# Packed attention and an expert layer on one core: weight staging in shared places, loads five pieces ahead, and PSUM pairs shared by h, W' and attention

## The chip, the core and the metric

The kernel runs on one core of one Trainium2 chip. The core has a matrix engine (TensorE, PE in the profile, with its weight loads as PEld), VectorE (DVE), ScalarE (ACT), GpSimd (POOL) and SyncE (SP), which here only issues DMA transfers. PE writes into PSUM, which has eight banks of 512 float32 values in each of 128 partitions; ACT and DVE read it from there. Every engine works through its own queue in order and waits on semaphores for the others. The metric is the device time of one execution in microseconds (us), and the number compared is the median of the runs.

## The reference

Batch 8, 8 heads, 576 tokens, head size 64, 32 packed queries a head. All inputs are float32 except the two weights, which reach the kernel as float64 (512 x 2048 and 2048 x 512).

```python
def sm_attn(qq, kk, vv):
    s = scale * np.matmul(qq, kk.transpose(0, 1, 3, 2))
    s = s - np.max(s, axis=-1, keepdims=True)
    a = np.exp(s)
    a = a / (np.sum(a, axis=-1, keepdims=True) + 1e-09)
    return np.matmul(a, vv)
p_packed = sm_attn(p, k, v)
out = sm_attn(q, p_packed, p_packed)
...
h = x @ w_in
sp = np.maximum(h, 0.0) + np.log1p(np.exp(-np.abs(h)))
g = h * erf(sp)
return (g @ w_out).astype(np.float32)
```

x is the attention's output with its heads side by side: 4608 tokens of 512 values.

## The kernel before

**Algebra.** The second attention of a batch has only 32 keys a head, so its output is never formed. `w_prime(b, j)` multiplies the packed values of batch b with 512 columns of w_in and gives W'; an h block then multiplies W' with the attention weights a2 of the batch. Float32 precision comes from splitting each factor into a high and a low float32r part and adding three products (`wph` x `a2h`, `wph` x `a2l`, `wpl` x `a2h`); the same holds for g x w_out (`woh`, `wol`, `gh`, `gl`).

**Units.** The work is cut into 128 units (b, c, i): batch b, half c of its tokens (288), and 256 of the 2048 hidden values (i of 8). `h_block` (lines 399 to 439) makes h of a unit: two halves k, each six matmuls into one PSUM bank, evicted by ACT. `o_block` (445 to 472) multiplies g by w_out and accumulates in four banks (`ps_o`) over the i of a segment; then ACT copies them out (L466) and a DMA writes them. For the first 32 units (batches 0 and 1, grouped) the gate is softplus and erf, each behind a table load, taken for two or three units at a time (lists `ENDS`, functions `begin_gates` and `end_gates`); h is copied at L417, and o runs five units behind h. For the other 96 the gate is a chain of tanh and square (L429 to L438), h is evicted at L419, and o runs three units behind. The first eight units use w_out whole, unsplit (`whole`).

**Weights.** A float64 piece of 128 x 512 comes by DMA into a staging tile of 4 KB a partition (L87). `begin` scales its upper words on ACT (L93), `end` repairs the bits with three DVE passes (L96 to L98). There are 16 pieces of w_in, `("wi", j, c)`, and 16 of w_out, `("wo", f)`; `split_w_out` (`"sp"`) later makes `woh` on ACT (L114) and `wol` on DVE (L115). Staging has two places (pool `stage`); the third to eighth load borrow places of the W' pool (`EARLY`), two more borrow places of a2. All loads, k, v, q and most output stores go through SP's queue.

**Order.** The opening is written out by hand (lines 582 to 655): attention of batch 0 (`first`, in the output banks) and of batch 1 (`second`) are generators that are stepped between weight conversions, filler matmuls (`keep_busy`) and the first four h blocks, and `keep_order` fixes that order on PE, DVE, ACT and SP. After it, `plan` says which conversions, attention steps, W' and splits are traced after which h block: `("wo", 4)` to `("wo", 7)` after h 4 and h 5, the others spread over h 7 to 16. From there the framework's scheduler orders each queue. In `do`, an item `"wi"` or `"wo"` issues its transfer and then at once traces its conversion.

**PSUM.** Eight banks: four in `ps_o`, two single ones in `ps_h` (one half of h each), and one pair in `ps_m`, used in turn by W' and by the attention's scores, transposes and packed output. The tile names in the profile are h, wp, s, t, p and o; `wos` and `wi` are staging tiles, `wo` and `w_in_sb` the float32 weights.

Of the kernel before, what the change touches and what calls it, by code (L numbers as in the profile page):

```python
# [28 lines left out]
def tile_pack_attention_moe(ctx: ExitStack, tc: tile.TileContext, qT, kT, v, pT, w_in, w_out, outT):  # L29
    nc = tc.nc  # L30
    P = 128
    B, _, NC, S = qT.shape
    DFF = w_in.shape[1]
    DM = w_out.shape[1]
    HT = S // 2
    NDM = DM // P
    FB = 512
# [16 lines left out]

    FIRST = {4: [("wo", 4), ("wo", 5)], 5: [("wo", 6), ("wo", 7)]}
    LATER = (7, 17)
    ENDS = (1, 3, 5, 7, 9, 12, 15, 18, 21, 24, 27, 29, 31)

    EARLY = ("wpl", "wpl", "wph", "wph", "wpl", "wpl")

    cpool = ctx.enter_context(tc.tile_pool(name="const", bufs=1))
    apool = ctx.enter_context(tc.tile_pool(name="attn", bufs=2))
    opool = ctx.enter_context(tc.tile_pool(name="wo", bufs=2 * (DFF // P) + 1))
    spool = ctx.enter_context(tc.tile_pool(name="stage", bufs=2))
    wpool = ctx.enter_context(tc.tile_pool(name="wp", bufs=NFB))
    tpool = ctx.enter_context(tc.tile_pool(name="tmp", bufs=3))
    ps_o = ctx.enter_context(tc.tile_pool(name="ps_o", bufs=1, space=bass.MemoryType.PSUM))
    ps_h = ctx.enter_context(tc.tile_pool(name="ps_h", bufs=2, space=bass.MemoryType.PSUM))
    ps_m = ctx.enter_context(tc.tile_pool(name="ps_m", bufs=1, space=bass.MemoryType.PSUM))

    ident = cpool.tile([P, P], F32, name="ident")
    bias = cpool.tile([P, 4], F32, name="bias")
    w_in_sb = cpool.tile([P, 4, DFF], F32, name="w_in_sb")
    wo, wo_hi, wo_lo = {}, {}, {}
# [2 lines left out]
    for i, c in enumerate((T_BIAS, Q_BIAS, U_BIAS, A_BIAS)):  # L77
        nc.vector.memset(bias[:, i:i + 1], c)

    def load_f32(dst, src, name, pool=None, tag="wst"):  # L80

        if src.dtype == F32:
            nc.sync.dma_start(dst, src)
            return (lambda: None,) * 2
        n = src.shape[1]
        st = (pool or spool).tile([P, n], I64, name=name, tag=tag)
        nc.sync.dma_start(st[:], src)  # L87
        words = st[:].bitcast(U32).rearrange("p (n two) -> p n two", two=2)
        low, high = words[:, :, 0], words[:, :, 1]
        bits = dst.bitcast(U32)  # L90

        def begin():
            nc.scalar.mul(dst, high.bitcast(F32), F64_SCALE)  # L93

        def end():
            nc.vector.tensor_scalar(bits, bits, 3, None, op0=ALU.logical_shift_left)  # L96
            nc.vector.scalar_tensor_tensor(bits, high, 0x80000000, bits, op0=ALU.bitwise_and, op1=ALU.bitwise_or)  # L97
            nc.vector.scalar_tensor_tensor(bits, low, 29, bits, op0=ALU.logical_shift_right, op1=ALU.bitwise_or)  # L98

        return begin, end  # L100

    def load_w_in(j, c, **slot):
        return load_f32(w_in_sb[:, c, j * FB:(j + 1) * FB], w_in[c * P:(c + 1) * P, j * FB:(j + 1) * FB],
                        f"wi{j}_{c}", **slot)

    def load_w_out(f, **slot):
        made = opool.tile([P, DM], F32, name=f"wo{f}", tag="wo")
        wo[f] = made
        return load_f32(made[:], w_out[f * P:(f + 1) * P, :], f"wos{f}", **slot)

    def split_w_out(f):
        hi = opool.tile([P, DM], F32R, name=f"woh{f}", tag="wo")
        lo = opool.tile([P, DM], F32R, name=f"wol{f}", tag="wo")
        nc.scalar.copy(hi[:], wo[f][:])  # L114
        nc.vector.tensor_tensor(lo[:], wo[f][:], hi[:], op=ALU.subtract)  # L115
        wo_hi[f], wo_lo[f] = hi, lo

    functions = []
# [11 lines left out]
    wp = {}  # L130
# [4 lines left out]
    def attention(b, roomy=False):  # L135
# [5 lines left out]
        def chunk(name, tag="kvq"):  # L141
            if tag == "kvq":
                return apool.tile([P, S], F32, name=f"{name}_{b}", tag="kvq", bufs=6)[:]
            return tpool.tile([P, S], F32, name=f"{name}_{b}", tag=tag)[:]

        def bank(name):

            if name in at_o:
                d = at_o[name]
                return [ps_o.tile([P, 512], F32, name=f"{name}_{b}_{x}", tag=f"ps_o{d + x}")[:] for x in range(2)], None  # L150
            ps = ps_m.tile([P, 2, 512], F32, name=f"{name}_{b}", tag="ps_m")
            return [ps[:, 0, :], ps[:, 1, :]], ps

        def copy_out(dst, banks, n):
# [10 lines left out]
        k = [chunk(f"k{c}") for c in range(NC)]  # L165
# [5 lines left out]
        for j in range(NCH):  # L171
            n = min(P, S - j * P)
            nc.sync.dma_start(values[j][0:n, 0:2 * NC * 64], v[b, j * P:j * P + n, :])
        yield
        q_at = ("t0", "t0", "t0", "t1") if roomy else ("kvq",) * NC
        q = []

        def load_q():
            q.extend(chunk(f"q{c}", q_at[c]) for c in range(NC))
            for c in range(NC):  # L180
                nc.sync.dma_start(q[c], qT[b, :, c, :])

        if b != 1:
            load_q()
            yield
        a1 = apool.tile([P, 2, S], F32, name=f"a1_{b}", tag="big", bufs=3)
        scores = []
        for c2 in range(2):
# [54 lines left out]
        for j in range(NCH):  # L243
            n = min(P, S - j * P)
# [7 lines left out]
        (nc.scalar.copy if roomy else nc.vector.tensor_copy)(ptt[:], po[:, 0:P])  # L252
        pt[b] = ptt
        yield
        if b == 1:
            load_q()
            yield
# [91 lines left out]
    def w_prime(b, j):  # L349

        hi = wpool.tile([P, 2, FB], F32R, name=f"wph{b}_{j}", tag="wph")
        lo = wpool.tile([P, 2, FB], F32R, name=f"wpl{b}_{j}", tag="wpl")
        ps = ps_m.tile([P, 2, 512], F32, name=f"wp{b}_{j}", tag="ps_m")
        for c in range(NC):
            for r in range(2):
                nc.tensor.matmul(ps[NK * c:NK * c + NK, r, :], pt[b][64 * r:64 * r + 64, NK * c:NK * c + NK],  # L356
                                 w_in_sb[64 * r:64 * r + 64, c, j * FB:(j + 1) * FB], start=True, stop=True)
        nc.scalar.copy(hi[:], ps[:])
        wp[b, j] = (hi, lo)
        return lambda: nc.vector.tensor_tensor(lo[:], ps[:], hi[:], op=ALU.subtract)  # L360
# [38 lines left out]
    def h_block(b, c, i, whole, n):  # L399


        grouped = n < GROUPED
        hs = tpool.tile([P, 2, HT], F32, name=f"hs{b}_{c}_{i}", tag="t1" if grouped and sum(n > e for e in ENDS) % 2 else "hs")
        for k in range(2):
            f = (2 * i + k) * P
            j, fo = f // FB, f % FB
            whi, wlo = wp[b, j]
            ps = ps_h.tile([P, 512], F32, name=f"h{b}_{c}_{i}_{k}", tag="ps_h")
            m = 0
            ahi, alo = a2[b]  # L410
            for r in range(2):
                for w, a in ((whi, ahi), (whi, alo), (wlo, ahi)):
                    nc.tensor.matmul(ps[:, 0:HT], w[:, r, fo:fo + P], a[:, r, c * HT:(c + 1) * HT],  # L413
                                     start=(m == 0), stop=(m == 5))
                    m += 1
            if grouped:
                nc.scalar.copy(hs[:, k, :], ps[:, 0:HT])  # L417
            else:
                nc.scalar.mul(hs[:, k, :], ps[:, 0:HT], 0.5)  # L419
        if grouped:  # L420
            group.append((hs, b, c, i, whole))
            if n in ENDS:
# [95 lines left out]
    for k, (b, j) in enumerate(uses):  # L518
# [5 lines left out]
        n = ready[b]  # L524
# [10 lines left out]
    conversions = [0]  # L535

    def fetch(what, *which, **slot):
        if not slot:
            conversions[0] += 1
        if not slot and 2 < conversions[0] <= 2 + len(EARLY):  # L540
            slot = dict(pool=wpool, tag=EARLY[conversions[0] - 3])
        return (load_w_in if what == "wi" else load_w_out)(*which, **slot)

    def do(items):
        for it in items:
            if it[0] == "att":
                b = it[1]
                if b not in gens:
                    gens[b] = attention(b)
                next(gens[b])  # L550
            elif it[0] == "sp":
                split_w_out(it[1])
            elif it[0] in ("wi", "wo"):
                for step in fetch(*it):
                    step()
            else:
                w_prime(it[1], it[2])()

# [24 lines left out]
    idle = ps_h.tile([P, 512], F32, name="idle", tag="ps_h")[:, 0:P]  # L583
    first, second = attention(0, roomy=True), attention(1)
    gens[1] = second
    next(first)
# [4 lines left out]
    next(second)  # L591
    wos = [fetch("wo", f) for f in range(4)]
    next(second)
    wis = [fetch("wi", 1, c) for c in range(2)]
    wis += [fetch("wi", 1, c, pool=apool, tag=tag) for c, tag in ((2, "a2h"), (3, "a2l"))]
    keep_busy(6, idle)
    next(first)
    next(first)
# [32 lines left out]
    next(first)  # L631
    wos[0][1]()
    h_block(*units[1][:3], True, 1)
    keep_busy(5, ps_m.tile([P, 2, 512], F32, name="idle2", tag="ps_m")[:, 0, 0:P])
    next(first)
    next(second)
    wos[1][1]()
# [11 lines left out]
    next(second)  # L649
    end = len(traced)  # L650
    with tc.high_priority():
        next(second)
        w_prime(0, 1)()
        for _ in range(4):
            next(second)
    behind = 1
    for n in range(len(units) + LAG):
        if 3 < n < len(units):
# [45 lines left out]
```

## Time and profile before

| what | before |
|---|---|
| median of 3 runs | 789.92 us |
| lowest and highest run | 786.32 and 792.06 us |
| span of the profiled execution | 786.2 us |
| mean granted clock of TensorE | 0.983 |
| bytes moved by DMA | 59.59 MB |

The span is that of one profiled execution, from the first to the last instruction of the program; no more of that execution's time is shown than this span, and it lies beside the lowest run. In the profile a row of the timeline has start, duration, engine, line, operation, output and inputs, shapes, how many were merged, and in brackets how long the engine stood idle before and whose end released it. A row of the windows view gives a stretch, its length, then for each engine the busy time and the number of instructions, and at the end the granted clock of TensorE, the DMA engines' share and GB/s. Matmuls are pipelined: the rows of a steady stretch overlap, so a matmul that is listed with 0.29 us starts 0.13 us after the one ahead of it.

### The profile page before, as it was taken

How to read it: one execution, taken by the hardware profiler on the slowest of the kernel's cores; microseconds unless marked ns; L12 is line 12 of the kernel's file. 1: busy time of each engine (PE TensorE's matmuls, PEld its weight loads, DVE VectorE, ACT ScalarE, POOL GpSimd, SP SyncE). 2: the span in 40 equal slices, each digit the busy share in tenths (PEclk: the TensorE clock that was granted, in tenths of full speed). 3: DMA queues.
4: the chain of work that ended last, by engine and by line, in shares of the span. 5: the costliest groups of instructions: out<-in, count | busy, mean ns of one | idle time of the engine just before them, and what ended most of it. 6: DMA issues, size and time to landing. Idle time of an engine off the chain costs nothing.

```text
span 786.2 us, 15369 instructions
## 1 busy us (share of the span) xinstructions
PE 749.0 (95%) x6354; PEld 672.7 (86%) x6354; DVE 564.2 (72%) x874; ACT 592.4 (75%) x994; POOL 22.7 (3%) x30
## 2 busy tenths in 40 slices
PE   7787958998999999999999999999999999999998
PEld 5475637778988999889998999899988999899998
DVE  4976766673376779766887669767897769766664
ACT  3676859777587778778687868778687868778784
POOL 0000110000111100000000000000000000000000
PEclk9998979999999999999999999999999999999999
DMA  8935562412442422002300221002400210000000
GB/s 303 348 121 177 137 141 81 138 50 61 106 88 32 83 78 72 16 2 85 132 31 1 83 76 65 25 1 80 133 31 2 80 47 4 29 1 32 1 32 31
DMA packets 32966, 59.59 MB, mean 76 GB/s; under 512 B 3712, under 2 KB 16000, under 8 KB 32896
## 3 DMA queue, kind: packets, MB, share of 16 engines
q1 hardware_dynamic: 29440, 55.06, 21.3%
q0 software_dynamic: 3456, 3.54, 3.8%
q8 instruction: 50, 0.82, 0.4%
q14 instruction: 20, 0.16, 0.1%
HBM read 45.61 MB, written 12.98 MB: 75 GB/s over the span
## 4 chain that ended last, share of the span: by engine, by line
PE 79%; ACT 9%; DMA 5%; DVE 4%; issue 2%; SPq 0%; ACTq 0%; DVEq 0%
PE o L459 46%; PE h L413 23%; DMA wos<-w_out 4%; PE wp L356 3%; PE p L247 2%; ACT L390 1%; PE s L192 1%; ACT t L390 1%; PE s L264 1%; ACT t L384 1%; ACT hs L417 1%; PE t L233 1%; DMA k<-kT 1%; ACT L384 1%; DVE wo L97 1%
## 5 line engine op out<-in xcount | busy, mean ns | idle before, releaser
L459 PE MATMUL o<-gl,woh 128*128 128x288 f32 x960 | 283.6, 296 | 1.3 <-DVE gl L369 1.3
L459 PE MATMUL o<-gh,woh 128*128 128x288 f32 x960 | 282.6, 300 | 0.0
L459 PE MATMUL o<-gh,wol 128*128 128x288 f32 x960 | 282.0, 295 | 0.0
L459 PEld LDWEIGHTS o<-gh,woh 128*128 128x128 f32 x960 | 178.4, 188 | 26.4 <-DVE t L433 10.2
L459 PEld LDWEIGHTS o<-gl,woh 128*128 128x128 f32 x960 | 180.6, 188 | 4.7 <-issue 2.6
L459 PEld LDWEIGHTS o<-gh,wol 128*128 128x128 f32 x960 | 180.8, 188 | 1.4 <-issue 1.4
L413 PE MATMUL h<-a2h,wph 128*128 128x288 f32 x512 | 155.8, 305 | 20.1 <-ACT hs L417 15.2
L413 PE MATMUL h<-a2l,wph 128*128 128x288 f32 x512 | 153.9, 301 | 1.7 <-DVE a2l L310 1.7
L413 PE MATMUL h<-a2h,wpl 128*128 128x288 f32 x512 | 153.9, 301 | 0.0
L419 ACT ACTIVATE hs<-h 128x288 f32<-128x288 f32 x192 | 77.9, 413 | 74.8 <-PE h L413 71.9
L413 PEld LDWEIGHTS h<-a2h,wph 128*128 128x128 f32 x512 | 98.5, 193 | 27.9 <-ACT hs L417 19.8
L438 DVE SCALAR_TENSOR_TENSOR hs<-t,hs 128x576 f32<-128x576 f32 x96 | 72.6, 756 | 55.5 <-ACT t L434 55.3
L413 PEld LDWEIGHTS h<-a2l,wph 128*128 128x128 f32 x512 | 98.5, 192 | 7.6 <-issue 3.8
L413 PEld LDWEIGHTS h<-a2h,wpl 128*128 128x128 f32 x512 | 98.5, 193 | 1.9 <-issue 1.9
L369 DVE TENSOR_TENSOR gl<-hs,gh 128x576 fp32r<-128x576 f32 x120 | 90.4, 754 | 1.3
L434 ACT ACTIVATE t<-t,bias 128x576 f32<-128x576 f32 x96 | 74.3, 774 | 19.4 <-DVE t L433 18.8
L368 DVE CAST gh<-hs 128x576 fp32r<-128x576 f32 x120 | 54.8, 457 | 45.0 <-PE o L459 43.2
L432 DVE SCALAR_TENSOR_TENSOR t<-t,hs 128x576 f32<-128x576 f32 x96 | 72.0, 749 | 15.2 <-ACT u L431 15.2
L429 ACT ACTIVATE t<-hs,bias 128x576 f32<-128x576 f32 x96 | 74.7, 778 | 2.3
L431 ACT ACTIVATE u<-t,bias 128x576 f32<-128x576 f32 x96 | 74.9, 780 | 1.8
L430 ACT ACTIVATE t<-t,bias 128x576 f32<-128x576 f32 x96 | 74.3, 774 | 1.5
L433 DVE SCALAR_TENSOR_TENSOR t<-u,t 128x576 f32<-128x576 f32 x96 | 72.3, 753 | 0.8
(79 smaller groups left out, 749.7 us busy)
## 6 DMA issues: line engine op xcount, KB each, us to landing
k<-kT SPq DMA_DIRECT2D x32, 288.0 KB, 4.5
q<-qT SPq DMA_DIRECT2D x32, 288.0 KB, 4.1
outT<-ob SPq DMA_DIRECT2D x64, 144.0 KB, 2.0
wi<-w_in SPq DMA_DIRECT2D x16, 512.0 KB, 5.8
v<-v SPq DMA_DIRECT2D x32, 256.0 KB, 3.6
wos<-w_out SPq DMA_DIRECT2D x16, 512.0 KB, 5.8
outT<-ob POOLq DMA_DIRECT2D x24, 144.0 KB, 4.8
v<-v SPq DMA_DIRECT2D x8, 128.0 KB, 4.3
```

The lines of the kernel that those rows point to most:

```text
L368: nc.vector.tensor_copy(ghi[:], hs[:])
L369: nc.vector.tensor_tensor(glo[:], hs[:], ghi[:], op=ALU.subtract)
L413: nc.tensor.matmul(ps[:, 0:HT], w[:, r, fo:fo + P], a[:, r, c * HT:(c + 1) * HT], start=(m == 0), stop=(m == 5))
L419: nc.scalar.mul(hs[:, k, :], ps[:, 0:HT], 0.5)
L429: nc.scalar.activation(t[:], hs[:], AF.Tanh, bias=bias[:, 0:1], scale=2.0 * T_SCALE)
L430: nc.scalar.activation(t[:], t[:], AF.Square, bias=bias[:, 1:2], scale=Q_SCALE)
L431: nc.scalar.activation(u[:], t[:], AF.Tanh, bias=bias[:, 2:3], scale=U_SCALE)
L432: nc.vector.scalar_tensor_tensor(t[:], t[:], 0.5 * A2, hs[:], op0=ALU.mult, op1=ALU.add)
L433: nc.vector.scalar_tensor_tensor(t[:], u[:], 0.5 * A1, t[:], op0=ALU.mult, op1=ALU.add)
L434: nc.scalar.activation(t[:], t[:], AF.Tanh, bias=bias[:, 3:4], scale=2.0 * A_SCALE)
L438: nc.vector.scalar_tensor_tensor(hs[:], t[:], 1.0, hs[:], op0=ALU.add, op1=ALU.mult)
L459: nc.tensor.matmul(acc[b, c][d][:, 0:HT], w[f][:, d * P:(d + 1) * P], gg[:, k, :], start=(first and k == 0 and n == 0), stop=(last and k = ...
```

## The change

Three things are changed together.

The pools `stage` and the borrowed places go. The pool `wo` now has 18 places of 4 KB in place of 33 of 2 KB; staging tiles, whole w_out pieces, the split pairs (high and low part in one tile) and q of batch 1 all take turns in it.

Transfers are separated from conversions. `fetch_ahead(n)` issues loads in the order of the plan until n of them are open; two are issued in the opening, and from the end of the opening on five are kept open, a new one after each conversion. q of batch 1 is loaded in the opening with the other loads, not after its packed attention.

`ps_h` and `ps_m` become one pool `ps_x` of two pairs of banks. h takes a pair for both halves; the 96 later units evict both halves with one ACT instruction, the 32 grouped ones still with two.

```diff
-    EARLY = ("wpl", "wpl", "wph", "wph", "wpl", "wpl")
+    AHEAD = 5
...
-    opool = ctx.enter_context(tc.tile_pool(name="wo", bufs=2 * (DFF // P) + 1))
-    spool = ctx.enter_context(tc.tile_pool(name="stage", bufs=2))
+    opool = ctx.enter_context(tc.tile_pool(name="wo", bufs=DFF // P + 2))
...
-    ps_h = ctx.enter_context(tc.tile_pool(name="ps_h", bufs=2, space=bass.MemoryType.PSUM))
-    ps_m = ctx.enter_context(tc.tile_pool(name="ps_m", bufs=1, space=bass.MemoryType.PSUM))
+    ps_x = ctx.enter_context(tc.tile_pool(name="ps_x", bufs=2, space=bass.MemoryType.PSUM))
...
-        st = (pool or spool).tile([P, n], I64, name=name, tag=tag)
+        st = opool.tile([P, n], I64, name=name, tag="wo")
...
-        hi = opool.tile([P, DM], F32R, name=f"woh{f}", tag="wo")
-        lo = opool.tile([P, DM], F32R, name=f"wol{f}", tag="wo")
+        both = opool.tile([P, 2, DM], F32R, name=f"wohl{f}", tag="wo")
+        hi, lo = both[:, 0, :], both[:, 1, :]
...
-        q_at = ("t0", "t0", "t0", "t1") if roomy else ("kvq",) * NC
...
-        if b != 1:
-            load_q()
-            yield
+        q_at = ("t0", "t0", "t0", "t1") if roomy else ("wo",) * NC if b == 1 else ("kvq",) * NC
+        q = [chunk(f"q{c}", q_at[c]) for c in range(NC)]
+        for c in range(NC):
+            nc.sync.dma_start(q[c], qT[b, :, c, :])
+        yield
...
-        ps = ps_m.tile([P, 2, 512], F32, name=f"wp{b}_{j}", tag="ps_m")
+        ps = ps_x.tile([P, 2, 512], F32, name=f"wp{b}_{j}", tag="ps_x")
...
+        ps = ps_x.tile([P, 2, 512], F32, name=f"h{b}_{c}_{i}", tag="ps_x")
         for k in range(2):
...
-            ps = ps_h.tile([P, 512], F32, name=f"h{b}_{c}_{i}_{k}", tag="ps_h")
...
             if grouped:
-                nc.scalar.copy(hs[:, k, :], ps[:, 0:HT])
-            else:
-                nc.scalar.mul(hs[:, k, :], ps[:, 0:HT], 0.5)
+                nc.scalar.copy(hs[:, k, :], ps[:, k, 0:HT])
+        if not grouped:
+            nc.scalar.mul(hs[:], ps[:, :, 0:HT], 0.5)
...
+    coming = [it for n in sorted(plan) for it in plan[n] if it[0] in ("wi", "wo")]
+    fetched = {}
...
+    def fetch_ahead(n):
+        while coming and len(fetched) < n:
+            it = coming.pop(0)
+            fetched[it] = fetch(*it)
...
             elif it[0] in ("wi", "wo"):
-                for step in fetch(*it):
+                for step in fetched.pop(it):
                     step()
+                fetch_ahead(AHEAD)
...
-    wis = [fetch("wi", 1, c) for c in range(2)]
-    wis += [fetch("wi", 1, c, pool=apool, tag=tag) for c, tag in ((2, "a2h"), (3, "a2l"))]
+    wis = [fetch("wi", 1, c) for c in range(4)]
+    next(second)
+    fetch_ahead(2)
...
         for _ in range(4):
             next(second)
+    fetch_ahead(AHEAD)
```

The filler matmuls' tiles (`idle`, `idle2`) move to `ps_x` as well.

More of the change, by code (lines that the diff above doesn't have):

```diff
@@ L78, in tile_pack_attention_moe, with load_f32 @@
         nc.vector.memset(bias[:, i:i + 1], c)
-    def load_f32(dst, src, name, pool=None, tag="wst"):
+    def load_f32(dst, src, name):
         if src.dtype == F32:
@@ L100, in load_f32, with load_w_in, load_w_out @@
         return begin, end
[L102 to L106, printed above, removed]
+    def load_w_in(j, c):
+        return load_f32(w_in_sb[:, c, j * FB:(j + 1) * FB], w_in[c * P:(c + 1) * P, j * FB:(j + 1) * FB], f"wi{j}_{c}")
+    def load_w_out(f):
         made = opool.tile([P, DM], F32, name=f"wo{f}", tag="wo")
         wo[f] = made
-        return load_f32(made[:], w_out[f * P:(f + 1) * P, :], f"wos{f}", **slot)
+        return load_f32(made[:], w_out[f * P:(f + 1) * P, :], f"wos{f}")
     def split_w_out(f):
-        hi = opool.tile([P, DM], F32R, name=f"woh{f}", tag="wo")
-        lo = opool.tile([P, DM], F32R, name=f"wol{f}", tag="wo")
-        nc.scalar.copy(hi[:], wo[f][:])
-        nc.vector.tensor_tensor(lo[:], wo[f][:], hi[:], op=ALU.subtract)
+        both = opool.tile([P, 2, DM], F32R, name=f"wohl{f}", tag="wo")
+        hi, lo = both[:, 0, :], both[:, 1, :]
+        nc.scalar.copy(hi, wo[f][:])
+        nc.vector.tensor_tensor(lo, wo[f][:], hi, op=ALU.subtract)
         wo_hi[f], wo_lo[f] = hi, lo
@@ L143, in chunk @@
                 return apool.tile([P, S], F32, name=f"{name}_{b}", tag="kvq", bufs=6)[:]
+            if tag == "wo":
+                return opool.tile([P, S], F32, name=f"{name}_{b}", tag="wo")[:]
             return tpool.tile([P, S], F32, name=f"{name}_{b}", tag=tag)[:]
@@ L150, in bank @@
                 return [ps_o.tile([P, 512], F32, name=f"{name}_{b}_{x}", tag=f"ps_o{d + x}")[:] for x in range(2)], None
-            ps = ps_m.tile([P, 2, 512], F32, name=f"{name}_{b}", tag="ps_m")
+            ps = ps_x.tile([P, 2, 512], F32, name=f"{name}_{b}", tag="ps_x")
             return [ps[:, 0, :], ps[:, 1, :]], ps
@@ L174, in attention @@
         yield
-        q_at = ("t0", "t0", "t0", "t1") if roomy else ("kvq",) * NC
[L176 to L181, printed above, removed]
-        if b != 1:
-            load_q()
-            yield
+        q_at = ("t0", "t0", "t0", "t1") if roomy else ("wo",) * NC if b == 1 else ("kvq",) * NC
[3 more added lines that the diff above has]
+        yield
         a1 = apool.tile([P, 2, S], F32, name=f"a1_{b}", tag="big", bufs=3)
@@ L254, in attention @@
         yield
-        if b == 1:
-            load_q()
-            yield
         nb = HT // NK
@@ L412, in h_block @@
                 for w, a in ((whi, ahi), (whi, alo), (wlo, ahi)):
-                    nc.tensor.matmul(ps[:, 0:HT], w[:, r, fo:fo + P], a[:, r, c * HT:(c + 1) * HT],
+                    nc.tensor.matmul(ps[:, k, 0:HT], w[:, r, fo:fo + P], a[:, r, c * HT:(c + 1) * HT],
                                      start=(m == 0), stop=(m == 5))
@@ L534, in tile_pack_attention_moe, with fetch @@
     gens = {}
[L535 to L542, printed above, removed]
+    coming = [it for n in sorted(plan) for it in plan[n] if it[0] in ("wi", "wo")]
+    fetched = {}
+    def fetch(what, *which):
+        return (load_w_in if what == "wi" else load_w_out)(*which)
+    def fetch_ahead(n):
+        while coming and len(fetched) < n:
+            it = coming.pop(0)
+            fetched[it] = fetch(*it)
     def do(items):
@@ L582, in tile_pack_attention_moe @@
     start = len(traced)
-    idle = ps_h.tile([P, 512], F32, name="idle", tag="ps_h")[:, 0:P]
+    idle = ps_x.tile([P, 2, 512], F32, name="idle", tag="ps_x")[:, 0, 0:P]
     first, second = attention(0, roomy=True), attention(1)
@@ L633, in tile_pack_attention_moe @@
     h_block(*units[1][:3], True, 1)
-    keep_busy(5, ps_m.tile([P, 2, 512], F32, name="idle2", tag="ps_m")[:, 0, 0:P])
+    keep_busy(5, ps_x.tile([P, 2, 512], F32, name="idle2", tag="ps_x")[:, 0, 0:P])
     next(first)
@@ L651, in tile_pack_attention_moe @@
     with tc.high_priority():
-        next(second)
         w_prime(0, 1)()
```

## The prediction

> **What bounds the kernel now.** I read the page's totals and its 40 slices first, then the windows view for the stretches that the slices set apart, and then the timelines of TensorE (PE) and ScalarE (ACT) where PE stands idle.
>
> ```profile
> span 786.2 us, 15369 instructions
> PE 749.0 (95%) x6354; PEld 672.7 (86%) x6354; DVE 564.2 (72%) x874; ACT 592.4 (75%) x994; POOL 22.7 (3%) x30
> ...
> PE   7787958998999999999999999999999999999998
> ```
> ```profile
> 0.00:44.00 44.00, 30.83 (x315) 22.12 (x315) 30.76 (x66) 23.86 (x47) 0.70 (x6) 0.95 0.83 291
> ...
> 62.00:76.00 14.00, 10.01 (x65) 6.90 (x64) 10.33 (x19) 8.65 (x16) 0.00 (x0) 0.80 0.59 191
> 76.00:100.00 24.00, 22.81 (x140) 16.65 (x140) 18.31 (x26) 18.39 (x29) 3.87 (x4) 0.97 0.52 131
> 100.00:122.00 22.00, 11.25 (x55) 7.34 (x53) 11.51 (x17) 13.79 (x24) 3.54 (x4) 0.77 0.54 130
> 122.00:200.00 78.00, 73.79 (x540) 64.42 (x541) 48.06 (x82) 61.79 (x104) 0.00 (x0) 0.98 0.25 76
> 200.00:700.00 500.00, 499.61 (x4482) 457.96 (x4482) 378.05 (x562) 392.67 (x652) 14.60 (x16) 1.00 0.19 54
> ```
>
> The windows rows give the stretch, its length, busy time and count of PE, weight loads, DVE, ACT and POOL, then the granted clock, the DMA share and GB/s. From 200 us on the kernel is PE and nothing else: 499.61 of 500 us at full clock. No saving on ACT, DVE or DMA can show there. What can be won lies ahead of 200 us, and in 62 to 122 PE is busy for only 10.01 + 22.81 + 11.25 = 44.1 of 60 us. The rows of PE at its idle places, and of ACT (which they name), say why:
>
> ```profile
> 67.66 0.40 PE L413 MATMUL h<-a2h,wph 128*128 128x288 f32 x1 [1.22 <-ACT wph L358]
> ...
> 69.81 0.72 PE L264 MATMUL s<-q,pt 64*32 64x288 f32 x16 [1.35 <-DVE wpl L360]
> ...
> 74.17 0.61 PE L413 MATMUL h<-a2h,wph 128*128 128x288 f32 x1 [1.43 <-ACT hs L417]
> ...
> 104.48 0.80 PE L413 MATMUL h<-a2h,wph 128*128 128x288 f32 x2 [2.85 <-ACT a2h L307]
> ...
> 114.92 0.61 PE L413 MATMUL h<-a2h,wph 128*128 128x288 f32 x1 [5.86 <-ACT hs L417]
> ```
> ```profile
> 66.04 0.66 ACT L93 ACTIVATE wo<-wos 128x512 f32<-128x512 f32 x1 [3.25 <-DMA wos<-w_out]
> 66.61 1.00 ACT L358 CAST wph<-wp 128x1024 fp32r<-128x1024 f32 x1
> ...
> 72.64 0.68 ACT L93 ACTIVATE w_in_sb<-wi 128x512 f32<-128x512 f32 x1 [1.40 <-DMA wi<-w_in]
> ...
> 101.69 0.66 ACT L93 ACTIVATE wo<-wos 128x512 f32<-128x512 f32 x1 [6.88 <-DMA wos<-w_out]
> ...
> 103.28 1.15 ACT L307 CAST a2h<-tb 128x1152 fp32r<-128x1152 f32 x1
> ...
> 113.93 0.66 ACT L93 ACTIVATE wo<-wos 128x512 f32<-128x512 f32 x1 [4.35 <-DMA wos<-w_out]
> 114.49 0.38 ACT L417 COPY hs<-h 128x288 f32<-128x288 f32 x1
> ...
> 115.71 1.28 ACT L384 ACT_TABLE_LOAD   x1
> ```
> ```profile
> 94.68 0.67 DVE L98 SCALAR_TENSOR_TENSOR w_in_sb<-wi,w_in_sb 128x512 uint32<-128x512 uint32 x1
> 95.42 15.56 SPq L87 DMA_DIRECT2D wos<-w_out  x4
> ...
> ACT wo L93 <- DMA wos<-w_out: 19.9, 7, 6.9
> ACT w_in_sb L93 <- DMA wi<-w_in: 4.9, 2, 3.5
> ...
> wos<-w_out SPq DMA_DIRECT2D x16, 512.0 KB, 5.8
> ```
>
> The reader is to see a chain of three links. ACT runs its queue in order; at its head stands a weight conversion (L93) that waits for a transfer; behind it stand the cast of W' (L358), of a2h (L307) or an eviction of h (L417), for which PE waits. The transfer is late because it is issued late: the staging pool has two places, and the load at 95.42 goes out when DVE's last pass over an earlier piece ends (94.68 + 0.67 = 95.35). Then it takes 6 us to land. Between 44 and 165 us ACT waits 19.9 + 4.9 = 24.8 us in that way (the waits view of that window).
>
> **The change part by part.** *Loads five pieces ahead.* Conversions, their count and their length stay (L93 and three DVE passes for each of 32 pieces); only the transfers are issued earlier. From h 4 on a load goes out while five conversions are still ahead of it. Conversions of this stretch start at 66.04, 72.64, 101.69, 113.93: some 6 to 8 us apart once the waits are taken out, so that being one piece ahead hides most of the 5.8 us of landing and two ahead hide all. So I cost the transfers at nothing; their cover is the conversions between, and without it the 24.8 us come back.
>
> What that is worth on PE: the first place has gaps of 1.22 + 1.35 + 1.43 = 4.0 us, the second 2.85 + 5.86 = 8.7. Each is also followed by matmuls at about half the rate:
>
> ```profile
> 74.17 3.25 PE h L413 x12
> ...
> 114.92 3.26 PE h L413 x12
> ...
> 308.97 1.60 PE h L413 x12
> ```
>
> These are pieces of the chain of waits; the granted clock of the two stretches stands in the windows above, 0.80 and 0.77. Twelve h matmuls take 3.25 instead of 1.60 us, twice: 3.3 us. Sum 4.0 + 8.7 + 3.3 = 16.0 us, which is also what lies between 60 us and the 44.1 that PE works.
>
> What is late next: ACT, with 8.65 + 18.39 + 13.79 = 40.8 us of work in these 60, and with gates that run as softplus, table load, erf, table load. The densest window of ACT that I find is 18.09 of 20 us, 90%:
>
> ```profile
> 260.00:280.00 20.00, 20.00 (x169) 19.25 (x162) 13.96 (x24) 18.09 (x33) 3.69 (x4) 1.00 0.40 81
> ```
>
> At 90% ACT needs 40.8 / 0.90 = 45.4 us, so at most 14.6 of the 60 can go. I take 13 (ACT at 87%), between that and 8.4, which are the gaps ended by a DMA alone (1.22, 2.85, and the 4.35 within 5.86). In 122 to 200 PE is busy 73.79 of 78 us, so the time won arrives there and is not given back; of ACT's DMA waits in it I count nothing.
>
> *The order on SP.* Up to the four pieces wi1 SP's queue keeps its order. Behind them come, new, the four q of batch 1 (moved ahead of its packed attention) and two pieces of w_out: four of 128x576 float32 and two of 128x512 eight-byte words, 2.2 MB, some 7.6 us at the 291 GB/s of the first 44 us. They share the engines with wi1, but ACT converts wi1 only at 44.57, and 40 to 44 us shows a DMA share of 0. Cost 0, at most 2 us. A fetch that waits for a place holds up what is queued behind it on SP: k and v of batch 2, whose first matmul comes at 171.79, and outT stores, on which four ob tiles and so ACT's L466 depend; the trace has one such wait of 0.97 us (61.54). Cost 0, at most 2.
>
> ```profile
> 44.57 2.41 ACT L93 ACTIVATE w_in_sb<-wi 128x512 f32<-128x512 f32 x4
> ...
> 61.54 0.41 ACT L466 COPY ob<-o 128x288 f32<-128x288 f32 x1 [0.97 <-DMA outT<-ob]
> ...
> 171.79 0.72 PE s L192 x16
> ```
>
> *18 places of 4 KB.* By h 4: four whole w_out (0 to 3), five loads (wo4 to wo7 take two places each, wi2 one) and q of batch 1: 4 + 9 + 4 = 17. It fits. By h 8: eight split pairs, four whole ones, wo8 to wo11 with their stages and one wi3: 8 + 4 + 8 + 1 = 21, three too many until the o blocks of units 6 and 7 end (100.6 us in this trace). The lead shrinks from five to three or so there, which is still more than the two that suffice.
>
> *Two pairs of PSUM banks for h, W' and attention.* An ungrouped unit evicts both halves of h at once: 96 times 2 x 413 ns against one 128x576, for which the copy of scores gives 624 ns. That takes 96 x 0.20 = 19 us off ACT, hidden by PE's 499.61 of 500; the chain of a unit starts 0.2 us later, hidden by a lag of three units. W' and attention now take turns with h. In steady state:
>
> ```profile
> L419 ACT ACTIVATE hs<-h 128x288 f32<-128x288 f32 x192 | 77.9, 413 | 74.8 <-PE h L413 71.9 <-DVE gl L369 2.2
> L158 ACT COPY a<-s 128x576 f32<-128x576 f32 x12 | 7.5, 624 | 0.8 <-PE s L192 0.8
> ...
> 304.56 1.02 PE wp L356 x16
> ...
> 313.77 1.60 PE h L413 x12
> ```
> ```profile
> 304.60 0.41 ACT L419 ACTIVATE hs<-h 128x288 f32<-128x288 f32 x1 [0.39 <-PE h L413]
> ...
> 308.17 1.19 DVE L360 TENSOR_TENSOR wpl<-wp,wph 128x1024 fp32r<-128x1024 f32 x1
> ```
>
> W' at 304.56 would take the second pair; the h at 308.97 needs the first, which is evicted at 305.01, and the h at 313.77 needs the second, free at 309.36. Margins of 4 us, so 0. Ahead of 200 us the second pair takes away 1.35 us (scores waiting for W's subtraction, counted above). In the first 44 us, where PE works 30.83, the second pair lets an h or a transpose go ahead of an eviction; attention 0 on DVE sets the pace there, so 0, at most 2 won. From above, an eviction of W' (0.99 us) per shared tile, priced as a rival.
>
> The row on the clock is 1.00 from 200 to 700 us although h already turns over its banks there. A rule that speaks against this part: the Trainium skill, "TensorE: Matmul & The Clock Gate", section "A second HAM failure mode: psum-queue depth-cycling", says of one kernel that turning over PSUM tiles made PE idle so briefly and so often that its clock swung between half and full. The trace before does not agree, but its h has banks of its own; by the row the sum stays as it is, by the rule it would be that of the last rival.
>
> Sum: 786.2 - 13 = 773.2 us for the profiled execution, whose span is next to the lowest of the runs (786.32). The median, 789.92, lies 3.7 above it, which would give 777. I say 775.
>
> **The rivals.** *ACT takes over* (0.13): the DMA waits go, but gates and table loads keep their pace, and only the gaps ended by a DMA alone go: 790 - 8.4 = 781. For it: each group of units costs ACT two table loads of 1.28 us (115.71) with its gates behind them. Against it: ACT idles 19 us of those 60.
>
> *The places run out* (0.14): fetches wait for places as they waited for staging, and the lead is none. Only the second pair's 1.35 us go, with some of the first place: 786 to 789. For it: 21 against 18. Against it: they end as soon as o blocks free whole w_out, and two ahead suffice.
>
> *Slower: h waits for a shared pair* (0.06): 24 W' and 36 attention tiles from 200 us on; where each holds up an h by half an eviction of W' (0.5 us), 60 x 0.5 = 30 us are lost: 775 + 30 = 805. It decides from 13 / 60 = 0.22 us per tile on. Against it: the margins of 4 us.
>
> *Slower by the clock* (0.02): each such tile also sends the next h to half clock, 60 x 1.65 = 99 us: 874. That is the page's rule on PSUM turnover at this kernel's prices.
>
> **How the numbers follow.** The forecast has 0.65, with 767 to 781 as its own range: 16 us and a little of what idles in 122 to 200 on the one side, 8.4 on the other, from the median. The measurement can tell about 1%, so faster means below 782.0: 0.65 and two thirds of the first rival, 0.09: 0.74. Same is the rest of it and the case of places: 0.04 + 0.14 = 0.18. Slower: 0.08. For 8 in 10 the range goes from 764 (all gaps and those of 122 to 200) up to 788 (the places).
>
> **What would show it.** Right: no wait of ACT's L93 for a DMA after 44 us above 1 us; the gaps at h 4 and at h 8 to 11 gone or below 2 us; the h that starts at 114.92 near 102; ACT above 80% up to 110 us; 200 us on with PE at 99% and clock 1.00. Wrong: L93 still waiting for wos (places), PE waiting for L419 or L360 in steady state (shared pairs), a window after 200 us below clock 1.00, or PE idle as long as before with ACT at softplus and erf.

## The result, and the profile after

| what | before | after |
|---|---|---|
| median | 788.8 us (4 runs) | 798.06 us (4 runs) |
| lowest and highest run | 786.32 and 792.06 us | 796.54 and 799.89 us |
| ratio after / before, 95% interval | | 1.0123 [1.0088, 1.0157] |
| span of the profiled execution | 786.2 us | 798.0 us |
| mean granted clock of TensorE | 0.983 | 0.971 |

The changed kernel is 1.2% slower, where 775 us and a gain of 2% were predicted. Four executions on record, one of the first staging alone (1422.72 us, the profiled one) and three of the kernel before (1026.43, 1430.8 and 2375.72 us), ran far slower than the rest and are in no ratio, though the medians of the next section count them. The totals and the slices of its page:

```profile
span 798.0 us, 15318 instructions
...
PE 751.2 (94%) x6354; PEld 676.4 (85%) x6354; DVE 566.7 (71%) x874; ACT 574.6 (72%) x897; POOL 22.2 (3%) x30
...
PE   6679498999999999999999999999999999999998
...
PEclk9779599999999999999999999999999999999999
```

The windows view of the same kernel, cut as before the change (stretch, length, busy time and count of PE, weight loads, DVE, ACT and POOL, granted clock, DMA share, GB/s):

```profile
62.00:76.00 14.00, 14.00 (x93) 10.03 (x86) 14.00 (x28) 8.31 (x17) 0.00 (x0) 1.00 0.77 249
76.00:100.00 24.00, 12.07 (x67) 7.91 (x66) 17.85 (x27) 16.21 (x24) 0.00 (x0) 0.65 0.31 106
100.00:122.00 22.00, 21.07 (x103) 16.21 (x103) 16.50 (x24) 15.84 (x27) 4.54 (x5) 0.92 0.49 102
...
200.00:700.00 500.00, 490.99 (x4384) 447.38 (x4382) 371.61 (x549) 369.21 (x558) 12.54 (x14) 1.00 0.19 54
```

The gaps in 62 to 76 and 100 to 122 us are filled: PE works 14.00 and 21.07 us there, where it worked 10.01 and 11.25. Two other stretches have lost. From 76 to 100 us PE now works 12.07 of 24 us at a clock of 0.65, where it worked 22.81 at 0.97. And from 200 us on, where PE had idled 0.39 of 500 us, it idles 9.01.

The waits views answer the prediction's first claim. ACT's waits for a DMA between 44 and 165 us are one row of 4.6 us in place of 19.9 + 4.9, and none is for w_out:

```profile
ACT w_in_sb L90 <- DMA wi<-w_in: 4.6, 3, 3.3
```

So all transfers but a few do come in time, and the kernel is slower all the same. These are PE's waits between 20 and 200 us in the kernel before (the first row) and in the changed kernel (two rows), and the changed kernel's from 200 us on (the last row): total, number of times, longest.

```profile
PE h L413 <- ACT hs L417: 15.2, 7, 5.9
...
PE h L402 <- ACT hs L406: 15.5, 12, 3.0
PE wp L345 <- ACT hs L406: 5.4, 1, 5.4
...
PE o L448 <- DVE gl L358: 8.6, 10, 1.2
```

With the staging alone, a run of the next section, the same view has 3.5 us (5 times, the longest 1.2) in place of the 15.2. With the shared pairs these waits for an eviction of h are back, 15.5 + 5.4 us, and now for another reason.

**The first place: one tile for both halves of a grouped h.** PE's rows in which it had stood idle, and ACT's ahead of them:

```profile
83.81 1.96 PE L345 MATMUL wp<-w_in_sb,pt 64*32 64x512 f32 x16 [5.36 <-ACT hs L406]
...
97.70 0.61 PE L402 MATMUL h<-a2h,wph 128*128 128x288 f32 x1 [3.04 <-ACT hs L406]
```
```profile
82.81 0.67 ACT L90 ACTIVATE w_in_sb<-wi 128x512 f32<-128x512 f32 x1 [3.34 <-DMA wi<-w_in]
83.38 0.39 ACT L406 COPY hs<-h 128x288 f32<-128x288 f32 x1
...
92.82 1.28 ACT L373 ACT_TABLE_LOAD   x1
...
94.82 1.28 ACT L379 ACT_TABLE_LOAD   x1
96.11 1.26 ACT L379 ACTIVATE t<-t 128x576 f32<-128x576 f32 x2
97.27 0.38 ACT L406 COPY hs<-h 128x288 f32<-128x288 f32 x1
```

W' at 83.81 waits for a pair that an h still holds. The copy that frees it, at 83.38, stands on ACT behind a conversion that waits 3.34 us for its transfer, so this wait has both the shared pair and a late transfer in it. PE's h at 97.70 starts when ACT's copy at 97.27 ends. That copy is the first half of the same unit, and it stands behind a pair of gates with two table loads of 1.28 us. Before the change the two halves lay in tiles of their own, and PE could write the second while ACT was busy. Now they are one tile, traced as write half 0, copy half 0, write half 1, and the second half's matmuls are held until the first half's copy has read the tile.

**The second place: attention.** PE's rows around h of units 52 and 53 (attention of batch 4; the rows left out are o and the other matmuls of h), one row of ACT, and the windows of 310 to 400 us:

```profile
365.39 1.04 PE L225 MATMUL t<-ident,a 128*128 128x128 f32 x8
366.26 0.38 PE L231 MATMUL p<-ident,a 128*64 128x128 f32 x2
...
370.07 0.30 PE L402 MATMUL h<-a2h,wph 128*128 128x288 f32 x1
...
370.43 2.64 PE L239 MATMUL p<-a1t,v 128*64 128x32 f32 x80
...
376.12 0.72 PE L253 MATMUL s<-q,pt 64*32 64x288 f32 x16
377.49 0.72 PE L253 MATMUL s<-q,pt 64*32 64x288 f32 x16
379.57 0.29 PE L402 MATMUL h<-a2h,wph 128*128 128x288 f32 x1
...
393.58 0.40 PE L448 MATMUL o<-gl,wohl 128*128 128x288 f32 x1 [1.20 <-DVE gl L358]
```
```profile
374.64 0.65 ACT L408 ACTIVATE hs<-h 128x576 f32<-128x576 f32 x1 [6.23 <-PE h L402]
```
```profile
310.00:350.00 40.00, 40.00 (x335) 36.38 (x333) 30.62 (x45) 31.50 (x47) 0.00 (x0) 1.00 0.05 16
350.00:400.00 50.00, 48.27 (x457) 44.52 (x456) 37.79 (x59) 35.44 (x56) 0.00 (x0) 1.00 0.27 86
```

t and p follow each other, then the two score tiles s. Each takes a pair, so twice in a row both pairs are attention's, and between the h that starts at 358.88 and the one at 379.57 there is only one, although a unit takes 5.6 us (422.7 us for the 76 units from 36 to 112 in the kernel before). PE has o matmuls to do meanwhile, but it uses up the three units of lead. ACT idles 6.23 us for want of an h; afterwards five h come in one burst (379.57 to 391.66), their gates bunch on ACT and DVE, and the o at 393.58 waits for gl. The stretch in which W' shares the pairs, 310 to 350 us, idles nothing.

### The profile page after: what moved, and what is told of

It reads as the page before. It is cut to its first block, busy times and chain, and to the rows that moved or that the text cites. A ratio compares the mean times of both kernels' runs of the same rounds, so it can differ in the third digit from the quotient of the medians.

```text
span 798.0 us, 15318 instructions
## 1 busy us (share of the span) xinstructions
PE 751.2 (94%) x6354; PEld 676.4 (85%) x6354; DVE 566.7 (71%) x874; ACT 574.6 (72%) x897; POOL 22.2 (3%) x30
## 4 chain that ended last, share of the span: by engine, by line
PE 75%; DVE 9%; ACT 8%; DMA 6%; issue 2%; SPq 0%; DVEq 0%; ACTq 0%
PE o L448 46%; PE h L402 20%; PE wp L345 3%; DMA wi<-w_in 3%; DMA q<-qT 2%; PE p L239 2%; PE s L253 1%; DVE t L422 1%; DVE hs L427 1%; DVE t L421 1%; PE s L184 1%; DVE ta L286 1%; DVE mx L283 1%; DVE gl L358 1%; ACT ta L280 1%
## 5 line engine op out<-in xcount | busy, mean ns | idle before, releaser
L448 PE MATMUL o<-gh,wohl 128*128 128x288 f32 x1920 | 406.9, 298 | 0.6 <-DVE gh L357 0.6
L448 PEld LDWEIGHTS o<-gh,wohl 128*128 128x128 f32 x1920 | 313.1, 188 | 28.7 <-DVE t L421 10.2
L448 PE MATMUL o<-gl,wohl 128*128 128x288 f32 x960 | 282.7, 297 | 8.6 <-DVE gl L358 8.6
L448 PEld LDWEIGHTS o<-gl,wohl 128*128 128x128 f32 x960 | 180.2, 188 | 14.5 <-DVE gl L358 10.9
L402 PE MATMUL h<-a2h,wph 128*128 128x288 f32 x512 | 158.0, 309 | 20.0 <-ACT hs L406 15.5
L408 ACT ACTIVATE hs<-h 128x576 f32<-128x576 f32 x96 | 62.5, 651 | 100.8 <-PE h L402 88.9
L349 DVE TENSOR_TENSOR wpl<-wp,wph 128x1024 fp32r<-128x1024 f32 x32 | 39.0, 1221 | 21.3 <-ACT wph L347 20.2
L406 ACT COPY hs<-h 128x288 f32<-128x288 f32 x64 | 24.9, 395 | 32.0 <-PE h L402 31.8
```

Source lines behind the costliest of these rows:

```text
L402: nc.tensor.matmul(ps[:, k, 0:HT], w[:, r, fo:fo + P], a[:, r, c * HT:(c + 1) * HT], start=(m == 0), stop=(m == 5))
L408: nc.scalar.mul(hs[:], ps[:, :, 0:HT], 0.5)
L448: nc.tensor.matmul(acc[b, c][d][:, 0:HT], w[f][:, d * P:(d + 1) * P], gg[:, k, :], start=(first and k == 0 and n == 0), stop=(last and k = ...
```

## The experiments

Theory A, of the expectations, puts the loss on the shared pairs, in the two places shown above (L406 in the expectations is the copy of a grouped h): the halves of a grouped h in one tile, and attention's tiles one behind the other. Its rivals put it on the staging (the places, the order of the loads) or on the single, later eviction of an ungrouped h.

Every median below is set against runs of the kernel before on the same chip: 787.48 us for the first run of the staging alone, the banks alone, the one copy and the pair each; 787.31 for the second run of the staging alone, two ahead and the two without t; 786.54 for the two with one step a unit. "The start of o of unit n" is counted in the timelines: twelve matmuls make an h, sixteen or twenty-four an o.

**The two parts, each alone.** The first kernel takes the staging and keeps the PSUM pools as they were; the second takes the pools and keeps the staging.

```diff
 # staging alone, against the changed kernel
-    ps_x = ctx.enter_context(tc.tile_pool(name="ps_x", bufs=2, space=bass.MemoryType.PSUM))
+    ps_h = ctx.enter_context(tc.tile_pool(name="ps_h", bufs=2, space=bass.MemoryType.PSUM))
+    ps_m = ctx.enter_context(tc.tile_pool(name="ps_m", bufs=1, space=bass.MemoryType.PSUM))
...
 # banks alone, against the kernel before
-    ps_h = ctx.enter_context(tc.tile_pool(name="ps_h", bufs=2, space=bass.MemoryType.PSUM))
-    ps_m = ctx.enter_context(tc.tile_pool(name="ps_m", bufs=1, space=bass.MemoryType.PSUM))
+    ps_x = ctx.enter_context(tc.tile_pool(name="ps_x", bufs=2, space=bass.MemoryType.PSUM))
...
```

> The staging and the loads ahead as in the changed kernel, PSUM as before (two single banks for h, one pair for W' and attention). Theory A (the loss is all PSUM: the second half of a grouped h waits for the copy of the first, and attention's t and p hold both pairs while h should run): the loads ahead are left with their gain, 770 to 782 us, PE at 99% or more from 200 to 700 us, o of unit 6 before 92 us. Theory B (the staging itself costs: loads moved up in the opening, 18 places too few): o of unit 6 stays near 110 us and the time at 788 us or more.

> The kernel before with only the two shared pairs of banks, one eviction for the two halves of an ungrouped h. Theory A: slower than the changed kernel, 800 to 812 us: both PSUM losses, and the waits for weight transfers still there; from 200 to 700 us PE is busy for about 491 us as in the changed kernel. Theory B: 786 to 792 us, as before.

Staging alone took 771.38 us, ratio 0.9786 [0.9732, 0.984]; banks alone 804.19 us, ratio 1.0197 [1.0138, 1.0256], with 490.91 of 500 us busy from 200 to 700. The loss belongs to the banks, and the loads ahead are a gain by themselves. The profile of the staging comes from its second run (there o of unit 6 starts at 92.69, where the first expectation had it before 92):

> The same program as the staging alone of the first run (shared places, loads five pieces ahead, PSUM as before), for a profile and a second interval. Theory A (the loads ahead remove the DMA waits, the shared pairs take back more): 770 to 775 us; in the trace no wait of ACT's conversions for a DMA above 2 us after 44 us, PE in 62 to 122 us busy for about 55 of 60 us where before has 44.1, and 499 or more of 500 busy from 200 to 700. Rival (the gain comes from something else, as fewer DVE or ACT collisions in the opening): the h of unit 8 starts no earlier than before's 104.48, and the time is won after 122 us.

It took 772.51 us, ratio 0.9822 [0.9792, 0.9853], span 770.5. Its windows, and its one row of ACT waiting for a DMA between 44 and 165 us:

```profile
62.00:76.00 14.00, 12.37 (x94) 9.42 (x90) 12.49 (x23) 10.25 (x19) 0.00 (x0) 1.00 0.71 240
76.00:100.00 24.00, 19.20 (x101) 13.47 (x101) 20.45 (x30) 20.58 (x32) 3.92 (x4) 0.93 0.38 89
100.00:122.00 22.00, 19.38 (x118) 13.96 (x117) 17.45 (x28) 18.61 (x31) 3.53 (x4) 0.92 0.57 149
122.00:200.00 78.00, 76.19 (x664) 70.37 (x664) 39.41 (x67) 58.15 (x101) 3.54 (x4) 1.00 0.21 56
200.00:700.00 500.00, 499.63 (x4421) 459.51 (x4421) 381.57 (x567) 397.53 (x661) 10.97 (x12) 1.00 0.18 51
```
```profile
ACT w_in_sb L91 <- DMA wi<-w_in: 8.3, 4, 2.9
```

From 62 to 122 us PE works 12.37 + 19.20 + 19.38 = 50.95 us, against 44.07 before: 6.9 us won, not the 55 of the expectation. h of unit 8 starts at 104.95 (before 104.48), so the rival was right on that point. But unit 9 starts 6.2 us earlier and unit 24 15.8 us earlier, and from there the lead stays at 15 to 16 us to the end. At least half of the gain comes after 122 us. The longest wait left, 2.9 us, is over the 2 us expected.

**Two ahead.**

```diff
-    AHEAD = 5
+    AHEAD = 2
```

> The staging alone again, with two loads kept open after the opening in place of five. My prediction held that two ahead hide all of the 5.8 us that a load takes to land: then the time is within 2 us of the staging alone (771 to 774). Rival (the depth of five counts, since conversions come in pairs and behind q, k and v of the next batch on the load queue): a third or more of the gain is lost, 776 to 785, with waits of ACT's conversions for w_in or w_out of 3 us or more between 60 and 125 us.

775.46 us, ratio 0.9855 [0.9821, 0.9889], between the range expected (771 to 774) and the rival's (776 to 785), with 9.8 us of waits for w_in (longest 3.6). The median is 2.95 us above that with five, a fifth of the gain; the profiled executions (771.1 and 770.5) lie closer, and the two intervals overlap. Two ahead give most of it; whether five give more isn't settled.

**One copy for a grouped h.** Both halves are written before one ACT copy evicts the pair.

```diff
-            if grouped:
-                nc.scalar.copy(hs[:, k, :], ps[:, k, 0:HT])
-        if not grouped:
+        if grouped:
+            nc.scalar.copy(hs[:], ps[:, :, 0:HT])
+        else:
             nc.scalar.mul(hs[:], ps[:, :, 0:HT], 0.5)
```

> The changed kernel, but a grouped h is also evicted by one copy after both halves, so that no matmul of its second half follows a copy from the same tile. Theory A: the waits of PE for L406 in the middle of an h block are gone, o of unit 6 comes 8 to 16 us earlier than its 113.8, and the time falls by 3 to 12 us to 786 to 795; from 200 to 700 us nothing changes (491 us busy). Theory B: no change in the first 100 us, 796 to 800 us.

798.75 us, ratio 1.0149 [1.0097, 1.0201]: no better than the change, as theory B had it, and PE works 485.99 of 500 us from 200 us on, where no change from 491 was expected. Yet the first place is mended. The waits for L406 between 20 and 200 us fall from 15.5 + 5.4 to 5.8 + 1.2 us, and o of unit 7 starts at 103.48 in place of 117.78. At unit 36 o is still 6.9 us ahead of the kernel before; at unit 37, the first attention of the ungrouped stage, the lead is 0.3 us. PE's row there:

```profile
299.34 1.33 PE L448 MATMUL o<-gh,wohl 128*128 128x288 f32 x4 [4.92 <-DVE gh L357]
```

**A pair each.** One pair for h, one for W' and attention, not shared; h still evicted as in the change.

```diff
-    ps_x = ctx.enter_context(tc.tile_pool(name="ps_x", bufs=2, space=bass.MemoryType.PSUM))
+    ps_h = ctx.enter_context(tc.tile_pool(name="ps_h", bufs=1, space=bass.MemoryType.PSUM))
+    ps_m = ctx.enter_context(tc.tile_pool(name="ps_m", bufs=1, space=bass.MemoryType.PSUM))
```

> The changed kernel with the two pairs not shared: one for h, one for W' and attention; the halves of a grouped h still wait for each other, and a grouped h now waits for the one before. To be read from 200 to 700 us. Theory A (turns): PE is back at 498 us or more of 500, and the units from 36 to 112 take 515 to 519 us as before (before: 273.6 to 696.4, 422.7; changed kernel 278.8 to 708.3, 429.5) in the way that their difference falls below 2 us. Theory C (the one late eviction of both halves delays the gate, and so o): PE stays near 491 us and the difference near 7 us. The first 100 us are as slow as in the changed kernel or slower.

845.04 us (two runs), ratio 1.0725 [1.0648, 1.0802]. Theory A missed both of its numbers: from 200 to 700 us PE works 490.99 us, which is the figure of theory C, and the units from 36 to 112 take 451.0 us (302.53 to 753.50) against 422.7 before (the 515 to 519 in the expectation are a slip). But the idle time in it lies ahead of 340 us (131.11 of 140 us worked), where grouped units still run up to 282 us. A window of 360 us in the ungrouped stage, the group of W' matmuls in it, and two rows of the timeline:

```profile
340.00:700.00 360.00, 359.88 (x3026) 314.78 (x3026) 261.62 (x389) 260.93 (x391) 0.00 (x0) 1.00 0.15 49
```
```profile
L346 PE MATMUL wp<-w_in_sb,pt 64*32 64x512 f32 x240 | 31.9, 601 | 0.0
```
```profile
355.43 1.04 PE L346 MATMUL wp<-w_in_sb,pt 64*32 64x512 f32 x2
...
358.19 1.08 PE L346 MATMUL wp<-w_in_sb,pt 64*32 64x512 f32 x14
```

PE idles 0.12 of 360 us, so one late eviction of both halves doesn't make it idle there, and theory C is out. But the order of the queue came out otherwise, with h between the W' matmuls, so the total says nothing on sharing; what it shows of W' stands at the end.

**Without t.** For batches 2 to 7 the transposes of t and their pair are left out; ACT copies as many values straight from a1, and the output is another one. The second kernel adds the one copy.

```diff
+        if b > 1:
+            nc.scalar.copy(a1t[:, 0:NT].rearrange("p (x j) r k -> p x (j r k)", x=2),
+                           a1[:].rearrange("p r s -> p (r s)")[:, 0:2 * 512].rearrange("p (x n) -> p x n", x=2))
+        else:
             banks = bank("t1")
...
```

> The changed kernel with one part left out for the batches 2 to 7: the eight transposes of t and their PSUM pair; ACT copies as many values straight from a1, so its time stays. The output is another. PE saves 8 x 0.11 us = 0.9 us a batch, 5 us in all, by every theory. Theory A (t and p, one behind the other, hold both pairs and keep h away for 64 o matmuls): h now comes between p's transposes and its product, the idle time of PE in 200 to 700 us falls from 9.0 to below 4 us, and the total to 785 to 789. Rival (the pairs are lost to scores and W' as much, or the one late eviction of h is at fault): idle stays at 7 to 9 us, total 792 to 794.

> The same without t's transposes, and with the grouped h evicted by one copy after both halves (as in the run with one copy), so both suspected causes are taken away at once while the pairs stay shared. Theory A: the 14.7 us that the one copy won at o of unit 7 are no longer given back in the attention phases: 774 to 781, near the staging alone less 5 us of work and some 10 for what sharing still costs the opening. Rival (the won time is given back for another reason, as ACT or DVE setting the pace of the ungrouped units): 790 or more, as without t's transposes alone.

Both missed: 808.01 us, ratio 1.028 [1.0245, 1.0315], and 800.98 us, ratio 1.0183 [1.0148, 1.0219], with less work than the change. The first rival missed too; the second one's time, 790 or more, came. PE works 482.89 and 482.54 of 500 us from 200 on. The rows of the first kernel name the next pair of neighbours:

```profile
379.75 1.40 PE L257 MATMUL s<-q,pt 64*32 64x288 f32 x32
```
```profile
384.97 0.65 ACT L412 ACTIVATE hs<-h 128x576 f32<-128x576 f32 x1 [6.18 <-PE h L406]
```

With t gone, the two s tiles stand back to back, 32 matmuls in one run, and hold both pairs until DVE has transposed them; ACT waits 6.18 us for an h as it waited 6.23 beside t and p in the changed kernel. The theory had named too few tiles. It isn't t and p alone, it is any two attention tiles with no h between, and they stand so because `plan_attention` spreads twelve steps over six units, two behind each h.

**One step a unit.** The changed kernel with one line of the plan altered, and the same with the one copy.

```diff
-        start, end = free, free + 6
+        start, end = free, free + STAGES - 1
```

> Without t, the two pairs were held by the next two tiles instead, the two of s2: they too stand back to back, since the plan puts an attention's 12 steps on six units, two behind each h. So theory A is put anew: any two attention tiles with no h between them shut h out. Here the changed kernel takes one step a unit (12 steps over 11 units), so that an h stands between any two of t, p and the s tiles; nothing else is changed and nothing left out. Theory A: the idle time of PE from 200 to 700 us falls from 9.0 to below 2 us, and the time to 787 to 791, the level of the kernel before, since the opening is as late as before. Rival (an attention tile of any place costs h a part of its eviction, so that the number of tiles counts and not their order): idle stays at 7 us or more, 795 to 800.

> The same order of attention, one step a unit, and the grouped h evicted by one copy after both of its halves. Theory A with both of its causes: with one copy, o of unit 36 started at 287.9 us against 294.8 before, and that lead was lost in the first attention behind it; here it stays: 777 to 782. Rival (the lead is lost elsewhere, to gates that come late because ACT and DVE set the pace up to 300 us): 786 or more.

787.52 us, ratio 1.0018 [1.0001, 1.0034], as the theory has it; with one copy 782.98 us, ratio 0.996 [0.994, 0.9979], 1 us above what was expected. Their windows from 200 to 700 us, in this order:

```profile
200.00:700.00 500.00, 498.96 (x4466) 456.45 (x4465) 380.10 (x561) 376.81 (x568) 11.64 (x13) 1.00 0.19 53
```
```profile
200.00:700.00 500.00, 498.25 (x4407) 458.13 (x4406) 382.53 (x562) 376.88 (x561) 11.39 (x13) 1.00 0.18 51
```

The idle time falls from 9.01 to 1.04 us with the same tiles in the same two pairs. The staging alone has the old order, with pairs that are not shared, and idles 0.37 us. So the loss takes both: sharing, and that order. One step a unit also spreads attention's work on ACT and DVE over more units, and no run tells this apart from the order of the tiles; in the staging alone that work is as bunched as in the change and costs PE nothing. Most of what still separates these two from the staging alone lies ahead of 200 us. The windows of the first 200 us of the kernel before, the staging alone, the change, one step a unit, and that with one copy, in this order:

```profile
0.00:200.00 200.00, 166.68 (x1254) 132.29 (x1255) 132.46 (x230) 137.94 (x238) 8.11 (x14) 0.93 0.49 153
```
```profile
0.00:200.00 200.00, 177.26 (x1432) 145.79 (x1433) 136.96 (x241) 145.02 (x252) 11.68 (x18) 0.95 0.52 163
```
```profile
0.00:200.00 200.00, 165.72 (x1257) 135.75 (x1257) 131.31 (x230) 136.73 (x238) 9.67 (x16) 0.89 0.48 153
```
```profile
0.00:200.00 200.00, 166.93 (x1281) 137.18 (x1282) 133.02 (x233) 140.09 (x242) 10.54 (x17) 0.91 0.49 155
```
```profile
0.00:200.00 200.00, 170.33 (x1388) 139.26 (x1389) 135.79 (x238) 140.89 (x223) 11.23 (x18) 0.95 0.51 162
```

The balance of the spans is then this. Loads ahead: 770.5 - 786.2 = -15.7 us. The shared pairs, with one step a unit: 784.7 - 770.5 = +14.2. Attention's order in the ungrouped stage: 798.0 - 784.7 = +13.3, of which 3.3 are there at o of unit 18 already (190.03 against 186.70), ahead of the altered steps, so that 10 belong to it. Together +11.8, which is 798.0 - 786.2. These are single executions, and four runs of the changed kernel lie up to 3.4 us apart; against the kernel before, the medians give -16.1 and -14.8 for the loads ahead, +1.0 for one step a unit and +9.3 for the change.

Of the 14.2 us, 9.8 are there at o of unit 18 (186.70 against 176.94); the other 4.4 come later, where PE idles hardly more than in the staging alone, and what they are was not tried. The one copy takes 6.5 us back in the spans (784.7 - 778.2) and 4.5 in the medians of ten runs each (787.52 - 782.98). Of the 7.7 that are left to the staging alone, 5.6 are there at o of unit 18 (182.50 against 176.94). For them the waits of that kernel between 20 and 200 us name the pair that W' holds until DVE has subtracted:

```profile
PE h L402 <- DVE wpl L349: 8.3, 3, 4.7
```

That this wait is what is left was not tried; it is read from the trace alone.

## Why the prediction was wrong, step by step

*Loads five pieces ahead: right, and alone worth what was said.* The waits for w_out are gone, and the staging alone took 771.4 and 772.5 us, inside the prediction's own range. The term of 13 us measured 15.7 in the spans, but its place was off. Idle time of PE in the first 200 us accounts for 177.26 - 166.68 = 10.6 of it: 6.9 in 62 to 122, 2.4 in 122 to 200 (76.19 against 73.79), of which nothing had been counted, and 1.3 earlier. The other 5 go with the clock by an estimate: its mean rose from 0.93 to 0.95, and 0.02 of 200 us is 4. The sum of 16.0, set beside the 15.9 us between 60 and 44.1, agreed by luck: its 3.3 us are rows in which PE works, slowly, so they lie within the 44.1, and the gaps that it lists are 12.7. The h that stood at 114.92 came to 108.75, not near 102.

*Two ahead suffice: nearly.* They keep four fifths of the gain or more. Waits for w_in above the 1 us of the prediction are left in both kernels, 2.9 us with five ahead and 3.6 with two. The conversions stand closer than the 6 to 8 us that were read: in the kernel before one starts at 67.89, behind that of 66.04.

*The order on SP and the 18 places: small in the staging alone, not nothing.* One transfer in the changed kernel, issued at 75.00, made ACT wait 3.34 us at 82.81, and W' on PE behind it 5.36 us; "at most 2" was too little there. The staging alone holds the 18 places and the moved loads of q as well and gains all the same, so the rival "the places run out" is out with its 786 to 789 us. Still, SP's queue there stands for 21.2 us ahead of one load in a row of four for w_in that begins at 73.07, and ACT waits 2.20 us for w_in at 100.93; whether that is a place was not tried, nor was the moved q by itself.

*Two pairs of PSUM banks, "Margins of 4 us, so 0": this step failed.* The margins were read where W' takes turns with h, and there they hold: 40.00 of 40 us busy from 310 to 350. But the pairs have three users, and attention's turns were not looked at, where two tiles follow each other with no h between. That is 10 us of the spans. For the first 44 us the prediction said "at most 2 won", and up to 200 us it counted only what a second pair takes away, 1.35 us of scores waiting for W'. It did not ask what one tile for both halves of a grouped h does when a copy is traced between them: 4.5 us by the medians, 6.5 by the spans, of the 14.2 that sharing still costs with attention spread. The 1.35 us didn't go away either: h waits for W' in place of the scores, 1.6 us in the changed kernel and 8.3 with one copy. The statement that ACT's 19 us saved are hidden was right: ACT works 574.6 us in place of 592.4, and no run shows a gain by it.

*The rivals.* "Slower: h waits for a shared pair" had 0.06 and is what came, by another mechanism than it was priced with. It charged each tile half an eviction, 60 times; measured, a W' tile costs nothing in steady state, and the loss goes by neighbours, once an attention. From 200 us on PE did not wait for an eviction of h or W' either: the wait that shows is o for gl, two steps behind the cause. "Slower by the clock" did not come: the clock of the changed kernel is 1.00 from 200 to 700 us, with ten waits of 1.2 us or less in it.

## What to carry to other kernels

When several kinds of tile are to share a rotation of buffers, write down the order in which they take it over a whole period, every user, and look for neighbours of the same kind: two long holders in a row shut the others out for both their lifetimes, and then a step of another kind between them can give the time back with no buffer added, as it did here. A tile that covers two banks is one tile: a copy of its first half, traced between the writes, orders the second write behind it. And measure the parts of a change alone: here one part gains 2% and the other takes more than that back.

## What the runs showed of the hardware

Some idle times of PE of less than 2.5 us cost it the full clock in these runs, others did not. PE's rows in the kernel without t, and the windows around; then a row of PE in the kernel before:

```profile
397.27 0.79 PE L452 MATMUL o<-gh,wohl 128*128 128x288 f32 x4 [1.87 <-DVE gh L361]
399.27 0.40 PE L452 MATMUL o<-gl,wohl 128*128 128x288 f32 x1 [1.21 <-DVE gl L362]
```
```profile
397.00:400.00 3.00, 1.52 (x8) 1.28 (x9) 3.00 (x6) 1.38 (x3) 0.00 (x0) 0.94 0.00 0
400.00:404.00 4.00, 4.00 (x27) 3.79 (x33) 2.08 (x4) 3.94 (x6) 0.00 (x0) 0.62 0.00 0
```
```profile
188.52 0.40 PE L413 MATMUL h<-a2h,wph 128*128 128x288 f32 x1 [2.44 <-ACT hs L417]
```

After 1.87 and 1.21 us of idling with 0.79 us of matmuls between, the window from 400 to 404 us has a mean clock of 0.62. One idle of 2.44 us by itself, in the last row, is followed by 4 us at 0.67, and one of 2.49 us at 183.37 in the kernel with the banks alone by 0.60. A single one of 1.93 us (139.06, in the kernel with one copy) was followed by 1.00, and so was the 1.20 us at 393.58 of the changed kernel. The Trainium skill, "TensorE: Matmul & The Clock Gate", section "Why this matters for your kernels", asks for no idle gap above some 3 us; in these rows no gap is that long, so in this case shorter ones were enough.

The W' matmuls, listed with 601 ns each on 64*32 of the array, overlap: sixteen in one run take 1.02 us (the row at 304.56 of the kernel before). In the kernel with a pair each, two of them alone took 1.04 us and the other fourteen 1.08. Splitting such a run costs as much as a second one: 31.9 us for 240 matmuls, or 2.1 for each sixteen, against 17.4 us for 256, or 1.1, from 310 to 670 us of the kernel before.
